# Token and channel mixing of the first two batches by halves, with the weight conversions spread further and the channel units set denser

## The chip, the cores and the metric

One core of a Trainium2 chip runs the whole program. The metric is device microseconds (us) of one execution.

## What is computed

Three layers follow one another on 4 batches of 448 tokens and 768 features (12 heads of 64). The reference, cut to its core:

```
attn = softmax(scale * q @ k^T, causal); x = attn @ v                # (4, 448, 768)
h  = relu(x^T @ w_tok1) @ w_tok2                                     # 448 -> 256 -> 448, over tokens
u  = x + h^T
x2 = u + relu(u @ w_ch1) @ w_ch2                                     # 768 -> 1536 -> 768, over channels
theta = x2 @ w_theta;  zr, zi = x2 * cos(theta), x2 * sin(theta)
y  = w_tok_r @ zr + w_tok_i @ zi
u2 = x2 + y
out = u2 + relu(u2 @ w_ch)
```

The weights arrive as 64-bit floats.

## The kernel before, in words

**Attention** runs in 168 steps: 4 batches, 6 pairs of heads, 7 score tiles each (`steps`). A step is a score matmul (L349, with L351 from the ninth pair on), a masked reduction on VectorE (L356), an exponential on ScalarE (L358), and later (LAG = 4 steps) the product with v (`pv`, L393 or L403). For pairs 0 to 11 the weights are transposed on TensorE (L365); from pair 12 (step 84) on they are split into two f16 parts (L378) and transposed by a DMA (L381, `pt<-ph`). After two pairs `tokmix` adds the token mixing and leaves two accumulator tiles `acc`; after six pairs a batch has its six.

**Channel units.** The layer `x2` is 96 units: for each batch and each half `fh` of the 1536 middle channels six units `ch1_unit` and six `ch2_unit`, in the order of the list `units`. A unit is 18 matmuls of 128x448 in f16 (L230 to L232, three products of a high and a low part), and needs one weight tile `ws` of 384 KB, loaded on SP's queue (L225, `stream_tile`) at most three units ahead. Units of a batch need its `ut` tiles: `split_ready` takes a power of two from the sum of squares of the six `acc` tiles (`power`: matmuls L136 and L138, two small VectorE operations, small GpSimd products L130 that give `p_u` and `s_u`), and then splits each `acc` (ScalarE L160 and VectorE L196). `UNIT_STEPS` says at which attention step each unit is written into the program; 69 units lie among the steps, the rest after them.

**Conversions.** 24 tiles of w_ch1 and w_ch2 are read as 64 bits (768 KB, tile `raw`, L173), rounded to f32 on VectorE (L183, L184, L185) after a ScalarE pass (L176, then squares L124), split in two f16 parts on GpSimd (L163) and VectorE (L196 `ws<-wf`) and stored for the units to load (`w_c<-ws`, L553). `ROUNDINGS` says at which step each begins; load, rounding, split and store come at fixed distances around that step. Six tiles of w_ch are converted late (`convert_late`). Conversions and units take their `ws` tiles from one ring of buffers.

The layer after it (`thetas`, `mix`, `out_unit`) follows the attention, mixed with the last units.

**Order.** Each engine executes its instructions in order; a scheduler sorts them by priority (`high_priority` moves an instruction forward) and by what they need, so that scores stand well ahead of the units that were written at the same step. SP's queue is one list as well: loads, stores and transposes start in its order.

Of the kernel before, what the change touches and what calls it, by code (L numbers as in the profile page):

```python
# [8 lines left out]
F32 = mybir.dt.float32  # L9
# [9 lines left out]
P = 128  # L19
B, H, S, D = 4, 12, 448, 64  # L20
E = H * D
NPR = H // 2
DT = E // P
# [2 lines left out]
FH = 6  # L26
NEG = -1.0e30
PSC = 32768.0
BUFS = dict(ut=12, h2=8, acc=12, ws=8, wf=3, raw=3, sb=3, ph=3, pt=5, t=3, junk=1)
NATIVE = {0, 1, 2, 3, 4, 5, 6, 7}  # L30
NATPV = {0, 1, 2, 3, 4, 5, 6, 7, 8, 9, 10, 11}
AHEAD, LAG, LOOK = 500, 4, 2
KEEP, UBACK = 6, 16
ROUND_BITS, ROUND_FETCH, ROUND_SPLIT, ROUND_STORE = 1, 2, 3, 5
LATE_CONVERT = 16
FIRST_UNIT, DENSE, RATE = 50, 88, (42, 29)
UNIT_STEPS = [FIRST_UNIT + n * (DENSE - FIRST_UNIT) // 14 if n < 14 else
              DENSE + -(-(n - 14) * RATE[0] // RATE[1]) for n in range(72)]
ROUNDINGS = [(at_step, n - 4) for n, at_step in enumerate((3, 4, 8, 9))] + [(14 + n * 78 // 23, n) for n in range(24)]
ENGINES = {  # L40
    0: dict(qhi="A", qlo="D", khi="A", klo="D", v="D", phi="A", xhi="A", xlo="D", uhi="A", ulo="D"),
}
# [12 lines left out]
def fused(ctx, tc, q, k, v, w_tok1, w_tok2, w_ch1, w_ch2, w_theta, w_tok, w_ch, out):  # L55
# [19 lines left out]
    main = ctx.enter_context(tc.tile_pool(name="main", bufs=2))  # L75
# [39 lines left out]
    p_w1, p_w2, p_wc = [table(f"p_w1{z}", 6) for z in range(2)], table("p_w2", 12), table("p_wc", 6)  # L115
# [13 lines left out]
    def product(dst, a, b, c):  # L129
        nc.gpsimd.tensor_scalar(out=dst, in0=a, scalar1=b, scalar2=c, op0=ALU.mult, op1=ALU.mult)  # L130

    def power(p, s, sq, unit=None):

        ps = mm_bank()
        n = sq.shape[-1]
        nc.tensor.matmul(ps[:, 0:1], lhsT=ones, rhs=tiny, start=True, stop=False)  # L136
        for j in range(n):
            nc.tensor.matmul(ps[:, 0:1], lhsT=ones, rhs=sq[:, j:j + 1], start=False, stop=j == n - 1)  # L138
        g = main.tile([P, 2], F32, tag="g", name="g", bufs=4)
        nc.vector.tensor_scalar(out=g[:, 0:1].bitcast(U32), in0=ps[:, 0:1].bitcast(U32), scalar1=1, scalar2=EXPONENT,  # L140
                                op0=ALU.logical_shift_right, op1=ALU.bitwise_and)
        two_over(g[:, 1:2], g[:, 0:1])
        product(s, g[:, 1:2], 2.0 ** -51, 1.0)
        if p is not None:
            product(p, g[:, 0:1], 2.0 ** 64, 1.0)
        if unit is not None:
            product(unit, g[:, 1:2], 2.0 ** -51, PSC)
# [304 lines left out]
    h2 = {}  # L452
# [2 lines left out]
    unit_end = [None]  # L455

    ready = set()

    def domain(b, fh):

# [22 lines left out]

    def ch2_unit(b, uT, acc, fh, d, w):
        ps = mm_bank()
        f = main.tile([P, 1], F32, tag="f", name="f", bufs=4)
        product(f, p_w2[:, fh * 6 + d:fh * 6 + d + 1], h_scale[0], 1.0)
        for ft in range(FH):
            unit_end[0] = mm3(ps[:, 0:S], w, h2[b, fh, ft], lambda a: a[:, ft * P:(ft + 1) * P], lambda a: a, ft == 0, ft == FH - 1)
        nc.vector.scalar_tensor_tensor(out=acc[d], in0=ps[:, 0:S], scalar=f, in1=acc[d], op0=ALU.mult, op1=ALU.add)  # L490
        if fh == 1:
            squares(sq_x[b][:, d:d + 1], acc[d])
            last_store[0] = nc.sync.dma_start(out=x2d[b][d], in_=acc[d])

    uTs = [[None] * DT for _ in range(B)]
    accs = [[None] * DT for _ in range(B)]
    units = [(b, fh, c, t) for b in range(B) for fh in range(2) for c in (1, 2) for t in range(6)]
    loaded = {}

    jobs = [((w_ch1, w_ch2)[c - 1][fh * 6 + t], wd[f"c{c}", fh, t],  # L500
             p_w1[fh][:, t:t + 1] if c == 1 else p_w2[:, fh * 6 + t:fh * 6 + t + 1]) for _, fh, c, t in units[:24]]
    late = [(w_ch[e], wd["c3", 0, e], p_wc[:, e:e + 1]) for e in range(DT)]

    def load_unit(n):
        if n < len(units) and n not in loaded and (n >= 24 or n in stored):
            b, fh, c, t = units[n]
            loaded[n] = stream_tile(wd[f"c{c}", fh, t])

    fetched, rounding, stored = {}, {}, set()
    at, halves = [0], [0]  # L510

    def split_ready():

        b = halves[0]
        if b < B and None not in accs[b]:
            s = s_u[:, b:b + 1]
            power(p_u[:, b:b + 1], s, sq_u[b])
            for d in range(DT):
                uTs[b][d] = hl_tile("ut")
                split_to(pick("uhi"), uTs[b][d], accs[b][d], s)  # L520
            halves[0] += 1
# [42 lines left out]
    def x_scale(b):  # L564
        power(p_x[:, b:b + 1], s_x[:, b:b + 1], sq_x[b])

    def run_units(n):
        for _ in range(n):
            u = at[0]
            load_unit(u)  # L570
            b, fh, c, t = units[u]
            if c == 1 and t == 0:
                h_scale[0] = domain(b, fh)
            if c == 1:
                ch1_unit(b, uTs[b], fh, t, loaded[u])
            else:
                ch2_unit(b, uTs[b], accs[b], fh, t, loaded[u])
            loaded[u] = None
            at[0] += 1
            for ahead in range(LOOK + (u >= 24)):  # L580
                load_unit(at[0] + ahead)
            if at[0] % 24 == 2 and 1 <= at[0] // 24 <= 3:
                x_scale(at[0] // 24 - 1)


    eng, turn = dict(ENGINES[0]), {}
# [392 lines left out]
```

## Time and profile before

| | |
|---|---|
| median of 3 runs | 893.53 us (893.36 to 894.15) |
| profiled execution | 893.95 us, of which 892.2 us is the span from the first to the last instruction |
| TensorE (PE) busy | 856.9 us, 96% |
| VectorE (DVE) busy | 631.9 us, 71% |
| ScalarE (ACT) busy | 543.7 us, 61% |
| granted TensorE clock, mean | 0.983 of full speed |

Matmuls are pipelined, so a matmul's own duration overlaps with the next one's, and a busy PE is not a PE at its peak. How fast PE works is read from the distance between the starts of consecutive matmuls.

### The profile page before, as it was taken

To read this page: it belongs to the slowest core of one execution; us is meant where nothing else is said; L and a number is where in the kernel's file an instruction comes from. 1 tells how busy PE (TensorE), PEld (TensorE's weight loads), DVE (VectorE), ACT (ScalarE), POOL (GpSimd) and SP (SyncE) were. 2 spreads that over 40 slices of the span, in tenths; PEclk is the share of its full clock that TensorE was granted. 3 is DMA by queue.
4 is the path that set the end of the run, shared out by engine and by line. 5 is a ranking of instruction groups with operands and counts; after the bars stand their busy time and mean duration, and the time that the engine had idled before them with its cause. 6 is when DMAs were issued, how large, how long until landed. Compare 5 with 4: busy or idle time off the path is not lost.

```text
span 892.2 us, 16092 instructions
## 1 busy us (share of the span) xinstructions
PE 856.9 (96%) x5619; PEld 551.0 (62%) x5619; DVE 631.9 (71%) x1511; ACT 543.7 (61%) x1271; POOL 180.9 (20%) x349
## 2 busy tenths in 40 slices
PE   7999789999979999999999989999999999999998
PEld 6888658786736656665656565555555555555554
DVE  6899957979998665767886358758856458566442
ACT  6798757767776663657664248447746447556441
POOL 2142322224142121211321111152111001101000
PEclk9999979999789999999999999999999999999999
DMA  7857846657699995767565679720621132231011
GB/s 225 250 181 236 289 168 215 238 198 220 150 337 300 289 213 145 187 165 179 150 194 146 188 248 303 241 72 20 193 89 56 60 115 62 72 116 57 18 50 73
DMA packets 105793, 149.63 MB, mean 168 GB/s; under 512 B 61104, under 2 KB 72304, under 8 KB 105712
## 3 DMA queue, kind: packets, MB, share of 16 engines
q1 hardware_dynamic: 105168, 147.59, 54.9%
q0 software_dynamic: 384, 0.79, 0.4%
q8 instruction: 44, 0.72, 0.3%
q10 hardware_dynamic: 160, 0.23, 0.1%
q14 instruction: 37, 0.30, 0.1%
HBM read 112.39 MB, written 22.81 MB: 152 GB/s over the span
## 4 chain that ended last, share of the span: by engine, by line
PE 71%; DVE 13%; DMA 8%; ACT 4%; issue 3%; POOL 2%; SPq 0%; DVEq 0%; ACTq 0%; POOLq 0%
PE ps_mm L230 16%; PE ps_mm L231 16%; PE ps_mm L232 16%; PE ps_pv L393 3%; PE ps_sc L349 3%; DMA ws<-w_c 3%; PE ps_sc L231 2%; PE ps_sc L230 2%; PE ps_sc L232 2%; DMA pt<-ph 2%; PE ps_mm L365 2%; DVE wf L184 1%; DVE sb L356 1%; PE ps_pv L403 1%; DVE ut L196 1%
## 5 line engine op out<-in xcount | busy, mean ns | idle before, releaser
L232 PE MATMUL ps_mm<-h,ws 128*128 128x448 f16 x432 | 152.1, 353 | 0.0
L231 PE MATMUL ps_mm<-h,ws 128*128 128x448 f16 x432 | 152.1, 353 | 0.0
L230 PE MATMUL ps_mm<-h,ws 128*128 128x448 f16 x432 | 151.6, 353 | 0.0
L230 PE MATMUL ps_mm<-ut,ws 128*128 128x448 f16 x288 | 104.5, 363 | 11.4 <-ACT ut L160 6.9
L230 PEld LDWEIGHTS <-ws 128*128 128x128 f16 x720 | 70.9, 98 | 69.3 <-DMA ws<-w_c 4.8
L232 PEld LDWEIGHTS <-ws 128*128 128x128 f16 x720 | 70.9, 99 | 65.4 <-issue 6.2
L358 ACT ACTIVATE sb<-sb,mx 128x192 f32<-128x192 f32 (+3 forms) x168 | 89.3, 533 | 35.5 <-DVE mx L356 31.5
L231 PEld LDWEIGHTS <-ws 128*128 128x128 f16 x720 | 70.8, 98 | 61.3 <-issue 4.3
L231 PE MATMUL ps_mm<-ut,ws 128*128 128x448 f16 x288 | 104.3, 362 | 1.2 <-DVE ut L196 1.2
L232 PE MATMUL ps_mm<-ut,ws 128*128 128x448 f16 x288 | 104.0, 361 | 0.0
L356 DVE CUSTOM_DVE_ANT_0 sb<-ps_sc,mask 128x192 f32<-128x192 f32 (+3 forms) x168 | 74.1, 454 | 13.5 <-PE ps_mm L365 10.1
L124 ACT ACTIVATE junk<-acc 128x448 bf16<-128x448 f32 x72 | 41.2, 572 | 63.8 <-DVE acc L871 40.8
L393 PE MATMUL ps_pv<-v_raw,ptf 128*128 128x128 f32 (+1 forms) x456 | 63.6, 277 | 1.0 <-DVE x L415 0.7
L160 ACT ACTIVATE ph<-sb 128x192 f16<-128x192 f32 (+3 forms) x84 | 36.2, 440 | 45.1 <-DMA pt<-ph 44.9
L378 DVE SCALAR_TENSOR_TENSOR ph<-sb,ph 128x64 f16<-128x64 f32 (+3 forms) x156 | 45.5, 335 | 25.6 <-ACT ph L160 25.2
L393 PEld LDWEIGHTS ps_pv<-v_raw,ptf 128*128 128x128 f32 x456 | 59.1, 193 | 6.0 <-PE ps_mm L138 1.5
L163 POOL TENSOR_SCALAR h<-t 128x448 f16<-128x448 f32 x48 | 33.0, 691 | 112.5 <-ACT t L476 107.0
L478 DVE TENSOR_TENSOR h<-t,h 128x448 f16<-128x448 f32 x48 | 32.0, 669 | 24.5 <-POOL h L163 24.5
L349 PE MATMUL ps_sc<-kh,qs 128*128 128x256 f32 (+2 forms) x112 | 45.7, 413 | 3.3 <-DVE mx L356 3.1
L130 POOL TENSOR_SCALAR f<-p_w,c_h 128x1 f32<-128x1 f32 x48 | 21.5, 450 | 126.7 <-DVE acc L490 91.6
L476 ACT ACTIVATE t<-ps_mm,c_scale 128x448 f32<-128x448 f32 x48 | 29.7, 621 | 28.3 <-PE ps_mm L232 25.2
L230 PE MATMUL ps_sc<-th,ut 128*128 128x384 f16 x144 | 47.0, 326 | 0.0
(215 smaller groups left out, 2096.1 us busy)
## 6 DMA issues: line engine op xcount, KB each, us to landing
ws<-w_c SPq DMA_DIRECT2D x120, 384.0 KB, 4.5
raw<-in_w_ch_dram SPq DMA_DIRECT2D x30, 768.0 KB, 5.0
w_c<-ws SPq DMA_DIRECT2D x30, 384.0 KB, 3.6
q_raw<-in_q_dram SPq DMA_DIRECT2D x16, 448.0 KB, 4.0
k_raw<-in_k_dram SPq DMA_DIRECT2D x16, 448.0 KB, 5.3
v_raw<-in_v_dram SPq DMA_DIRECT2D x24, 288.0 KB, 3.3
x2d<-acc SPq DMA_DIRECT2D x24, 224.0 KB, 3.1
acc<-x2d SPq DMA_DIRECT2D x24, 224.0 KB, 3.1
```

Source lines behind the costliest of these rows:

```text
L124: nc.scalar.activation(j[:, 0:src.shape[-1]], src, AF.Square, accum_out=dst)
L160: nc.scalar.activation(dst, src, AF.Copy, scale=scale)
L163: e.tensor_scalar(out=dst, in0=src, scalar1=scale, scalar2=0.0, op0=ALU.mult, op1=ALU.add)
L230: nc.tensor.matmul(ps, lhsT=ka(a[:, 0]), rhs=kb(b[:, 0]), start=first, stop=False)
L231: nc.tensor.matmul(ps, lhsT=ka(a[:, 0]), rhs=kb(b[:, 1]), start=False, stop=False)
L232: return nc.tensor.matmul(ps, lhsT=ka(a[:, 1]), rhs=kb(b[:, 0]), start=False, stop=last)
L349: nc.tensor.matmul(ps[:, 0:n], lhsT=lhs, rhs=cut(pp.kh), start=True, stop=pp.kl is None)
L356: pp.first = nc.vector.tensor_tensor_reduce(out=dst, in0=src, in1=msk, op0=ALU.add, op1=ALU.min, scale=-0.125, scalar=3.0e38, accum_out=pp ...
L358: pp.last = nc.scalar.activation(sb[:, 0:kk], sb[:, 0:kk], AF.Exp, bias=pp.mx[:, j:j + 1], scale=-1.0, accum_out=pp.sm[:, j:j + 1])
L378: nc.vector.scalar_tensor_tensor(out=dst, in0=sb[:, c0:c1], scalar=PSC, in1=hi[:, c0:c1], op0=ALU.mult, op1=ALU.subtract)
L393: pp.pv = nc.tensor.matmul(pp.ps[:, reg:reg + n], lhsT=pt[:, u], rhs=pp.v[0][:, vt * D:vt * D + n], start=(u == 0), stop=(u == len(blks) - 1))
L478: gates[0] = nc.vector.tensor_tensor(out=t[:, 1], in0=f, in1=t[:, 0], op=ALU.subtract)
```

## The change

- The units of batches 0 and 1 run by halves: batch 0 first half, batch 1 first half, batch 0 second half, batch 1 second half (`HALVES`). Batches 2 and 3 stay as they were. The second half's weights are therefore needed 12 units later.
- The 24 conversions begin at steps 14 to 111 (`CONVERTED`) where they began at steps 14 to 92.
- 12 units stand at steps 53 to 89, 36 at steps 93 to 131, 21 at steps 135 to 165. Before, 14 stood at steps 50 to 87 and one every 1.45 steps from step 88 on.
- 16 buffers for `acc` where there were 12; 7 for `ws` where there were 8; 2 for `raw` where there were 3.
- `split_ready`'s `power` gets high priority, and from batch 1 on the six scales `f` of a half are one GpSimd product.

```diff
-BUFS = dict(ut=12, h2=8, acc=12, ws=8, wf=3, raw=3, sb=3, ph=3, pt=5, t=3, junk=1)
+BUFS = dict(ut=12, h2=8, acc=16, ws=7, wf=3, raw=2, sb=3, ph=3, pt=5, t=3, junk=1)
...
-ROUNDINGS = [(at_step, n - 4) for n, at_step in enumerate((3, 4, 8, 9))] + [(14 + n * 78 // 23, n) for n in range(24)]
+FIRST_UNIT = 53
+UNIT_STEPS = [FIRST_UNIT + n * 10 // 3 for n in range(12)] + [93 + n * 11 // 10 for n in range(36)] + [135 + n * 3 // 2 for n in range(21)]
+CONVERTED = [14 + 6 * n for n in range(6)] + [49 + 5 * n for n in range(6)] + [78 + n * 19 // 5 for n in range(6)] + [99 + n * 5 // 2 for n in range(6)]
...
+HALVES = ((0, 0), (1, 0), (0, 1), (1, 1), (2, 0), (2, 1), (3, 0), (3, 1))
...
-        f = main.tile([P, 1], F32, tag="f", name="f", bufs=4)
-        product(f, p_w2[:, fh * 6 + d:fh * 6 + d + 1], h_scale[0], 1.0)
+        if b == 0:
+            f = main.tile([P, 1], F32, tag="f", name="f", bufs=4)
+            product(f, p_w2[:, fh * 6 + d:fh * 6 + d + 1], h_scale[0], 1.0)
+        else:
+            if d == 0:
+                f_six[0] = main.tile([P, DT], F32, tag="f6", name="f6", bufs=2)
+                product(f_six[0], p_w2[:, fh * 6:fh * 6 + 6], h_scale[0], 1.0)
+            f = f_six[0][:, d:d + 1]
...
-    units = [(b, fh, c, t) for b in range(B) for fh in range(2) for c in (1, 2) for t in range(6)]
+    units = [(b, fh, c, t) for b, fh in HALVES for c in (1, 2) for t in range(6)]
...
-            power(p_u[:, b:b + 1], s, sq_u[b])
+            with tc.high_priority(AHEAD):
+                power(p_u[:, b:b + 1], s, sq_u[b])
...
-            if at[0] % 24 == 2 and 1 <= at[0] // 24 <= 3:
-                x_scale(at[0] // 24 - 1)
+            if u >= 2 and units[u - 2][1:] == (1, 2, 5):
+                x_scale(units[u - 2][0])
```

`load_unit` and `jobs` follow the new order: a unit's weights are loaded once the conversion of that tile is stored.

Three places show the order that results. The first is VectorE's list just ahead of the first unit, around the first splits into `ut` (the `ws<-wf` rows are the ends of conversions, `wf` alone is rounding). Before:

```order
L196 SCALAR_TENSOR_TENSOR ws_1368<-wf_1224,s_1369,ws_1368 128x768
L183 TENSOR_SCALAR wf_1524<-wf_1524 128x768
L410 TENSOR_TENSOR x0_188<-ps_pv_1282,sm_1174 128x384
L415 TENSOR_SCALAR x0_188<-ps_pv_1282,sm_1174 64x64 x2
L184 SCALAR_TENSOR_TENSOR wf_1524<-raw_1210,wf_1524 128x768
L140 TENSOR_SCALAR g_1407<-ps_mm_1399 128x1
L185 SCALAR_TENSOR_TENSOR wf_1524<-raw_1210,wf_1524 128x768
L127 TENSOR_SCALAR g_1407<-g_1407 128x1
...
L196 SCALAR_TENSOR_TENSOR ws_1471<-wf_1364,s_1472,ws_1471 128x768
L196 SCALAR_TENSOR_TENSOR ut_1412<-acc_579,s_u_149,ut_1412 128x448
```

and now:

```order
L411 TENSOR_TENSOR x0_188<-ps_pv_1188,sm_1101 128x384
L141 TENSOR_SCALAR g_1301<-ps_mm_1293 128x1
L416 TENSOR_SCALAR x0_188<-ps_pv_1188,sm_1101 64x64 x2
L168 TENSOR_TENSOR qs_1523<-q_raw_1517,qs_1523 64x896
L197 SCALAR_TENSOR_TENSOR ws_1268<-wf_1143,s_1269,ws_1268 128x768
L128 TENSOR_SCALAR g_1301<-g_1301 128x1
...
L168 TENSOR_TENSOR xg1_1405<-x0_188,xg0_1404 128x4x128
L197 SCALAR_TENSOR_TENSOR ut_1306<-acc_569,s_u_149,ut_1306 128x448
```

The whole rounding of a tile (`wf_1524`) and the end of one more conversion have left this place; in the list up to the first `ut` split 11 conversions were complete and now 6 are.

The second is GpSimd's list at the same place, where `s_u` is the scale that the splits wait for. Before:

```order
L130 TENSOR_SCALAR p_u_148<-g_1407 128x1
L130 TENSOR_SCALAR c_h_1487<-p_fh_147,p_u_148 128x1
L130 TENSOR_SCALAR f_2083<-p_w2_143,c_h_1487 128x1
L130 TENSOR_SCALAR f_2169<-p_w2_143,c_h_1487 128x1
L130 TENSOR_SCALAR f_2249<-p_w2_143,c_h_1487 128x1
L130 TENSOR_SCALAR f_2408<-p_w2_143,c_h_1487 128x1
L130 TENSOR_SCALAR s_u_149<-g_1407 128x1
```

and now:

```order
L131 TENSOR_SCALAR c1_scale0_145<-p_w10_141,two_fh0_1437 128x6
L131 TENSOR_SCALAR p_u_148<-g_1301 128x1
L131 TENSOR_SCALAR c_h_1441<-p_fh_147,p_u_148 128x1
L131 TENSOR_SCALAR s_u_149<-g_1301 128x1
L131 TENSOR_SCALAR p_w2_143<-g_1418 128x1
```

Four products `f` no longer stand ahead of `s_u`.

The third is SP's queue where the last of the 24 conversions (`w_c2_1_5`) is stored and loaded again by a unit. Before:

```order
L553 DMA w_c2_1_5_116<-ws_3322 128x1536
L493 DMA x2d0_0_69<-acc_579 128x448
L381 DMA_TRANSPOSE pt_3709<-ph_3705 128x7x128
L381 DMA_TRANSPOSE pt_3755<-ph_3751 128x7x128
L493 DMA x2d0_1_70<-acc_596 128x448
L225 DMA ws_3498<-w_c2_1_5_116 128x1536
```

and now:

```order
L226 DMA ws_4075<-w_c2_1_3_114 128x1536
L565 DMA w_c2_1_4_115<-ws_4038 128x1536
L501 DMA x2d0_0_69<-acc_569 128x448
L382 DMA_TRANSPOSE pt_4659<-ph_4655 128x5x128
L174 DMA raw_6093<-in_w_ch_dram 128x1536
L501 DMA x2d0_1_70<-acc_586 128x448
L226 DMA ws_4213<-w_c2_1_4_115 128x1536
L565 DMA w_c2_1_5_116<-ws_4147 128x1536
L226 DMA ws_4333<-w_c2_1_5_116 128x1536
```

The load that served the 24th unit now serves the 36th, and it stands directly behind the store it reads.

## Rows read from the trace of the kernel before

**Rows 1.** The page's head: span, then busy time of two engines.

```profile
span 892.2 us, 16092 instructions
PE 856.9 (96%) x5619; PEld 551.0 (62%) x5619; DVE 631.9 (71%) x1511; ACT 543.7 (61%) x1271; POOL 180.9 (20%) x349
```

**Rows 2.** PE's timeline: start, length, line, tiles, idle before and its releaser.

```profile
112.80 0.53 PE L230 MATMUL ps_mm<-ut,ws 128*128 128x448 f16 x1 [4.67 <-ACT ut L160]
...
115.97 0.53 PE L231 MATMUL ps_mm<-ut,ws 128*128 128x448 f16 x1 [1.20 <-DVE ut L196]
...
116.67 0.58 PE L230 MATMUL ps_mm<-ut,ws 128*128 128x448 f16 x1
117.04 0.58 PE L231 MATMUL ps_mm<-ut,ws 128*128 128x448 f16 x1
...
123.55 0.35 PE L232 MATMUL ps_mm<-ut,ws 128*128 128x448 f16 x1
123.74 0.35 PE L230 MATMUL ps_mm<-ut,ws 128*128 128x448 f16 x1
...
354.96 0.35 PE L230 MATMUL ps_mm<-h,ws 128*128 128x448 f16 x1
```

**Rows 3.** Busy time by stretch, with granted clock, DMA share and rate.

```profile
core 0: us, PE busy (x) PEld busy (x) DVE busy (x) ACT busy (x) POOL busy (x), PEclk, DMA share, GB/s
0.00:20.00 20.00, 15.19 (x86) 12.54 (x87) 12.94 (x49) 12.94 (x37) 5.33 (x17) 1.00 0.79 235
20.00:100.00 80.00, 76.93 (x551) 67.06 (x550) 74.59 (x191) 65.18 (x178) 24.39 (x38) 1.00 0.70 230
100.00:120.00 20.00, 13.40 (x74) 8.77 (x73) 17.02 (x39) 16.58 (x38) 7.75 (x13) 0.78 0.83 291
120.00:220.00 100.00, 100.00 (x692) 77.07 (x691) 77.70 (x192) 67.16 (x168) 30.41 (x46) 0.99 0.60 201
220.00:260.00 40.00, 30.28 (x216) 21.01 (x214) 38.00 (x98) 32.08 (x78) 12.31 (x18) 0.81 0.82 219
260.00:340.00 80.00, 78.51 (x596) 50.24 (x595) 60.45 (x172) 45.40 (x118) 15.35 (x31) 0.99 1.02 273
540.00:892.20 352.20, 347.65 (x1987) 192.08 (x1985) 219.04 (x427) 192.29 (x382) 47.90 (x103) 1.00 0.30 97
```

**Rows 4.** The same view, from the start to one point each.

```profile
0.00:112.80 112.80, 99.52 (x689) 85.46 (x690) 98.44 (x266) 89.11 (x241) 36.10 (x67) 0.99 0.74 237
0.00:340.00 340.00, 314.31 (x2207) 236.69 (x2208) 280.71 (x737) 239.33 (x614) 95.53 (x162) 0.96 0.77 234
```

**Rows 5.** Groups by line and shape: what one conversion costs; busy, mean ns, idle before.

```profile
L196 DVE SCALAR_TENSOR_TENSOR ws<-wf,s,ws 128x768 f16<-128x768 f32 x30 | 30.7, 1023 | 8.9 <-POOL ws L163 6.9 <-ACT ws L160 1.8
L184 DVE SCALAR_TENSOR_TENSOR wf<-raw,wf 128x768 uint32<-128x768 uint32 x30 | 30.2, 1006 | 0.3
L185 DVE SCALAR_TENSOR_TENSOR wf<-raw,wf 128x768 uint32<-128x768 uint32 x30 | 29.1, 971 | 0.2
L183 DVE TENSOR_SCALAR wf<-wf 128x768 uint32<-128x768 uint32 x30 | 20.4, 680 | 1.4 <-ACT wf L176 1.2
L176 ACT ACTIVATE wf<-raw 128x768 f32<-128x768 f32 x30 | 27.3, 910 | 3.6 <-DVE ws L196 3.5
L124 ACT ACTIVATE junk<-wf 128x768 bf16<-128x768 f32 x30 | 25.2, 838 | 3.4 <-DVE wf L185 2.8 <-DVE g L127 0.4
```

**Rows 6.** GpSimd's timeline at the first unit.

```profile
110.43 1.47 POOL L130 TENSOR_SCALAR f<-p_w,c_h 128x1 f32<-128x1 f32 x4
111.86 0.19 POOL L130 TENSOR_SCALAR s_u<-g 128x1 f32<-128x1 f32 x1
```

**Rows 7.** The chain that ended last, around unit 16.

```profile
246.34 10.03 DMA ws<-w_c
```

**Rows 8.** DMA issues: count, KB each, median us from issue to landing.

```profile
ws<-w_c SPq DMA_DIRECT2D x120, 384.0 KB, 4.5
w_c<-ws SPq DMA_DIRECT2D x30, 384.0 KB, 3.6
```

More of the change, by code (lines that the diff above doesn't have):

```diff
@@ L35 @@
 LATE_CONVERT = 16
-FIRST_UNIT, DENSE, RATE = 50, 88, (42, 29)
-UNIT_STEPS = [FIRST_UNIT + n * (DENSE - FIRST_UNIT) // 14 if n < 14 else
-              DENSE + -(-(n - 14) * RATE[0] // RATE[1]) for n in range(72)]
-ROUNDINGS = [(at_step, n - 4) for n, at_step in enumerate((3, 4, 8, 9))] + [(14 + n * 78 // 23, n) for n in range(24)]
+FIRST_UNIT = 53
+UNIT_STEPS = [FIRST_UNIT + n * 10 // 3 for n in range(12)] + [93 + n * 11 // 10 for n in range(36)] + [135 + n * 3 // 2 for n in range(21)]
+CONVERTED = [14 + 6 * n for n in range(6)] + [49 + 5 * n for n in range(6)] + [78 + n * 19 // 5 for n in range(6)] + [99 + n * 5 // 2 for n in range(6)]
+ROUNDINGS = [(at_step, n - 4) for n, at_step in enumerate((3, 4, 8, 9))] + [(at_step, n) for n, at_step in enumerate(CONVERTED)]
+HALVES = ((0, 0), (1, 0), (0, 1), (1, 1), (2, 0), (2, 1), (3, 0), (3, 1))
 ENGINES = {
@@ L457, in fused @@
     ready = set()
+    f_six = [None]
     def domain(b, fh):
@@ L496, in fused @@
     accs = [[None] * DT for _ in range(B)]
-    units = [(b, fh, c, t) for b in range(B) for fh in range(2) for c in (1, 2) for t in range(6)]
+    units = [(b, fh, c, t) for b, fh in HALVES for c in (1, 2) for t in range(6)]
     loaded = {}
     jobs = [((w_ch1, w_ch2)[c - 1][fh * 6 + t], wd[f"c{c}", fh, t],
-             p_w1[fh][:, t:t + 1] if c == 1 else p_w2[:, fh * 6 + t:fh * 6 + t + 1]) for _, fh, c, t in units[:24]]
+             p_w1[fh][:, t:t + 1] if c == 1 else p_w2[:, fh * 6 + t:fh * 6 + t + 1])
+            for fh in range(2) for c in (1, 2) for t in range(6)]
     late = [(w_ch[e], wd["c3", 0, e], p_wc[:, e:e + 1]) for e in range(DT)]
     def load_unit(n):
-        if n < len(units) and n not in loaded and (n >= 24 or n in stored):
-            b, fh, c, t = units[n]
+        if n >= len(units) or n in loaded:
+            return
+        b, fh, c, t = units[n]
+        if fh * 12 + c * 6 - 6 + t in stored:
             loaded[n] = stream_tile(wd[f"c{c}", fh, t])
```

## The prediction

> **What bounds the kernel now.** The page's head comes first: PE is busy 96% of the span [rows 1], which seems to leave nothing to win. [...] I counted every matmul at its spacing at full clock: 2664 of this kind at 0.189 us make 503.5, 504 of 384 columns at 0.162 make 81.6, 816 f32 ones of 128 columns at about 0.11 make 89, and the remaining 1635 small ones make 109 us. PE's work is therefore 783.7 us, and 108.5 us of the span are lost: PE stood, was fed thinly, or ran at half clock. I call this "lost time", and follow it by the start of each unit (18 matmuls, 3.4 us).
>
> When unit 0 starts, at 112.8, PE has done 61.9 us of work, so 50.9 are lost. When unit 35 starts, at 354.96 [rows 2], it has done 262.6, so 92.3 are lost. By unit 75 it is 103.0, and only 5.4 come after. From 540 on VectorE (DVE) has 219 us of work in 352 and PE loses almost nothing [rows 3]. So the tail cannot be improved, and everything is decided in the first 355 us.
>
> The table of stretches says what holds PE up there [rows 3]. From 20 to 100 DVE is busy 74.6 of 80 us: it is the bound, with ACT at 65.2. At 100 to 120 DVE is busy 17.0 of 20; PE waits 4.67 and 1.20 us for the `ut` splits [rows 2] and runs at half clock behind that (0.78 in the row). From 120 to 220 DVE has slack, 77.7 of 100, and PE is the bound. From 220 to 260 DVE is the bound again, 38.0 of 40, and PE gets too little; a wait of 10.03 us for a weight load ends this stretch [rows 7]. So the load alternates: DVE is full while PE starves, and then the reverse.
>
> **The change, part by part.** *Conversions.* One costs DVE 0.68 + 1.01 + 0.97 + 1.02 = 3.68 us and ACT 0.91 + 0.84 = 1.75 us, small operations aside [rows 5]. Five fewer of them are complete ahead of unit 0: DVE is relieved of 18.4 us there, ACT of 8.7. DVE had 98.4 us of work by 112.8, ACT 89.1 [rows 4]. As DVE was the bound, up to 18 us of time could go; as ACT takes part in the same steps and then becomes the busier of the two, it may be only 9. I take 13.
>
> *The scale `s_u`.* Four products of 1.47 us together leave the place ahead of it [rows 6], and its matmuls rank higher. That is 1.5 us of the wait, and up to 5 us more if PE's standing becomes too short to lose the clock. I take 3 in all.
>
> *`acc`, `f` in one product, `HALVES`.* 16 buffers hold two batches and two thirds of a third; GpSimd, which has the fewer and larger products, is busy 181 us of 892 [rows 1]. Both cost nothing. The cover of the buffers is that batch 0 is finished (unit 35) before the third mixing of batch 2 needs its tiles; if not, `tokmix` waits one unit, 3.4 us.
>
> *From unit 2 on.* I sum DVE's work in its new order, each instruction at its mean duration. (Done for the kernel before, this count gives the measured 98.4 at unit 0.) Batch 1's splits, which unit 12 needs, end at 193 us of DVE work; the last of the 24 conversions ends at 281. In the kernel before they ended at 223 and at 236. To get the time, DVE's idle time is added. Up to unit 12 I expect 7.1 idle in the first 20 us, as now [rows 3]; 10 up to unit 0, against 5.4 now, as ACT shares the bound (bounds 5 and 16); 3 around unit 0, as in 100 to 120; 8 in the 92 us of work up to unit 12, where DVE has more to do than PE (92 against 81): between the 5% idle of 220 to 260 [rows 3] and the 17% of the first 340 us [rows 4]. That is 28, so unit 12 starts at about 193 + 28 = 221 us. PE has then done 156.6, so 64 are lost; the kernel before had lost about 75 at that much work.
>
> *From unit 12 to unit 35.* PE has 105 us of work here, DVE 88. At the end unit 35 waits for the last conversion: a store of 3.6 and a load of 4.5 us [rows 8] behind DVE's 281, so 97 in all. PE's 105 is the larger, and the usual small gaps add 4: 109 is one end. The other end is the DMA. SP's queue holds, between the loads of units 12 and 35, 23 unit loads, 11 stores, 11 `raw` loads, 15 loads of q, k and v, 2 stores of x2 and 36 transposes: 33.9 MB, where it held 31.5. The row that comes nearest to a full DMA moved 273 GB/s at a share of 1.02 [rows 3]; at that rate 33.9 MB take 124 us. [...] The row is one of mixed transposes, as this stretch is, but the trace does not show that it could not have gone faster, so I take 114, one third of the way: unit 35 starts at about 335, with 73 us lost against 92.3 now.
>
> *After unit 35.* PE has 522 us of work left, and I leave the losses as they are: 10.7 up to unit 75 and 5.4 behind. That is 335 + 522 + 16 = 873 us of span. The profiled execution took 893.95, 1.75 more than its span, and the median of the runs is 0.42 below that one; so the forecast is **874.5 us**, 19 us (2.1%) less. Of these, 16 come ahead of unit 2 (13 + 3), 5 are given back up to unit 12, where DVE is the bound, and 8 to 9 are won from there to unit 35, where PE now lost 14 or more, the long wait for weights among them.
>
> **The rivals.** *The DMA fills (slower than forecast, still faster than before).* From unit 12 to 35 the stretch takes 124 to 130 us. For it: the share of 1.02, and the 10.03 us landing behind three `raw` loads [rows 7]. Against it: two `raw` buffers let fewer loads pile up. Time: 884 to 891.
>
> *ACT holds the first stretch.* Only 5 of the 16 us ahead of unit 2 come: 885. Against it: ACT was at 65 of 80 with the conversions still in it [rows 3].
>
> *Better.* DVE idles 20 up to unit 12 and the second stretch takes its 109: 861.
>
> *Slower than before: the ring of `ws`.* It has 7 buffers, and unit loads now come three ahead in a dense row of 36 units, between which 11 conversions want a buffer each for their split. A conversion that finds none holds GpSimd (L163) and then DVE (L196), with the masked reductions of the scores queued behind it on DVE, so that PE loses its scores too. With 8 buffers the splits of 30 conversions waited 8.9 us on DVE in all [rows 5], which speaks against it. If each of the 11 waits for one unit, 3.4 us, that is 37 us: 912. It decides from six such waits on (20 us).
>
> *Slower by the clock.* PE gets only 50 us of work in some 80 us before unit 12 is dense. [...] If the clock were low throughout, these 50 us would take 100: 895. [...]
>
> **How the numbers follow.** Forecast case (866 to 883): 0.50. DMA or ACT (883 to 892): 0.21. Better (below 866): 0.12. No measurable change: 0.04. Slower: 0.13, of which the ring 0.09 and the clock 0.04. A measurement of this kernel tells 0.2% (1.8 us) from no change. Faster is 0.50 + 0.21 + 0.12 = 0.83. The best bounds (unit 12 at 212, 109 behind it, the rest as now) give 861, the worst that still win 892. The range 859 to 892 leaves some 0.05 below and 0.15 to 0.17 above.
>
> **What the profile would show.** Right: unit 0 starts near 98 to 102 with ACT above 85% ahead of it; no wait of 4 us for `ut`; unit 12 near 221; unit 35 near 335; no loss in the tail. DMA: waits of PE for `ws<-w_c` of several us between 220 and 340 at a share near 1. Ring: idle time of L163 and L196 on `ws` of 20 us or more. Clock: a row of 0.5 to 0.8 between 170 and 250. The prediction is wrong above all if the losses after unit 35 do not stay at 16: PE then runs some 20 us ahead, and DVE, which must finish batch 2's splits before unit 48, has that much less time.

## The result, and the profile after

The changed kernel takes 900.84 us (median of 5 runs, 898.67 to 903.62); the kernel before took 893.72 beside it. The ratio is 1.0084 (95%: 1.0064 to 1.0104): slower by 0.8%, where 874.5 us and faster were forecast. The profiled execution took 900.77 us. Medians here and below are of all executions, while the ratios leave out one slow execution each of `e1_conv_old` (991.82 us; the other five have a median of 905.59) and of `p3_before_natpv14` (3141.0 us). The head of the profiled execution's page has, as before [rows 1], one span and the busy times:

```profile
span 898.9 us, 16042 instructions
PE 856.7 (95%) x5619; PEld 550.2 (61%) x5619; DVE 633.0 (70%) x1511; ACT 544.2 (61%) x1271; POOL 168.6 (19%) x319
```

The work is the same; the span is 6.7 us longer, and PE stands for it. The table of stretches shows where (columns as in [rows 3] and [rows 4]):

```profile
0.00:20.00 20.00, 14.60 (x83) 12.10 (x84) 12.72 (x48) 13.32 (x37) 5.35 (x17) 1.00 0.66 197
20.00:100.00 80.00, 76.16 (x555) 67.79 (x553) 57.98 (x167) 60.61 (x169) 15.99 (x25) 1.00 0.53 167
100.00:120.00 20.00, 19.75 (x132) 14.62 (x133) 19.92 (x51) 18.05 (x47) 8.45 (x12) 1.00 0.79 265
120.00:220.00 100.00, 95.86 (x696) 75.83 (x695) 82.94 (x209) 73.06 (x183) 21.08 (x38) 0.98 0.67 211
220.00:260.00 40.00, 31.33 (x239) 19.33 (x237) 37.79 (x103) 28.25 (x72) 12.43 (x20) 0.83 0.85 223
260.00:340.00 80.00, 74.56 (x490) 44.34 (x491) 65.83 (x154) 41.64 (x95) 23.98 (x39) 0.94 0.90 259
540.00:898.90 358.90, 352.06 (x2013) 194.36 (x2012) 224.84 (x437) 197.98 (x394) 46.78 (x96) 1.00 0.31 101
0.00:109.47 109.47, 100.06 (x707) 87.84 (x708) 80.09 (x243) 82.79 (x229) 26.22 (x51) 1.00 0.59 182
0.00:231.97 231.97, 211.44 (x1511) 174.17 (x1511) 185.44 (x506) 173.74 (x455) 55.83 (x101) 0.97 0.63 198
```

From 20 to 100 DVE has 16.6 us less to do than before, and PE gains nothing there. From 100 to 120 the gain is real: PE busy 19.75 for 13.40, the clock at 1.00 for 0.78. From 120 on it is given back: 4 us of standing by 220, and a clock of 0.83 until 260, 0.81 before; from 260 to 340 0.94 for 0.99.

PE's timeline after, to set against [rows 2]: the first line is unit 0, the last two are units 12 and 35.

```profile
109.47 0.36 PE L231 MATMUL ps_mm<-ut,ws 128*128 128x448 f16 x1
...
205.11 0.20 PE L404 MATMUL ps_pv<-v_hi,pt 128*128 128x64 f16 x1 [2.25 <-DMA pt<-ph]
...
225.04 0.21 PE L404 MATMUL ps_pv<-v_raw,pt 128*128 128x64 f16 x1 [2.87 <-DVE v_raw L318]
...
230.86 0.24 PE L404 MATMUL ps_pv<-v_hi,pt 128*128 128x64 f16 x1 [3.06 <-DMA pt<-ph]
...
231.97 0.97 PE L231 MATMUL ps_mm<-ut,ws 128*128 128x448 f16 x2
...
355.64 0.35 PE L231 MATMUL ps_mm<-h,ws 128*128 128x448 f16 x1
```

Unit 0 starts without the wait of 4.67 us. Unit 10 starts at 197.10, unit 11 at 217.15 and unit 12, batch 1's first, only at 231.97: PE has little but attention steps in this time, and they wait, longest for their transposes. I call this the hole. PE's waits from 190 to 262, with their sum, number and longest:

```profile
PE ps_pv L404 <- DMA pt<-ph: 6.6, 5, 3.1
PE ps_pv L404 <- DVE v_raw L318: 2.9, 1, 2.9
PE ps_sc L350 <- DVE mx L357: 2.0, 4, 0.9
PE ps_pv L404 <- DVE x L416: 0.9, 1, 0.9
```

These waits make 12.4 us. The half clock seen in this time (from 235.2 to 236.7 the granted clock was 0.50 and f16 matmuls of 128x448 started 0.37 us apart, from 237.4 to 239 1.00 and 0.19; a mean of 0.87 from 190 to 262, row below) costs up to 0.13 x 72 = 9 us more, an estimate, and less where PE waits anyway.

**Lost time, counted again.** I redid the prediction's count with a spacing for every kind of matmul: the lower quartile of the distances between starts in the kernel before. PE's work is 823.5 us in both kernels, not 783.7, so before lost 69 us in all and not 108.5. Time lost at the same amount of PE work:

```
PE work done     100   170   220   302 (unit 35)   end
before          27.1  28.6  48.2  53.0             68.7
after           17.0  19.7  45.5  54.7             75.4
```

The change wins 10.1 us by 100 us of work, gives 7.4 back by 220, 4.4 more by unit 35 and 5.1 behind it: together the 6.7 of the spans. The mark at 220 lies on a jump of the changed kernel, and finer marks show where the time is given back. The hole costs 18.7 us up to unit 13 (180 to 200 us of work), as much as the kernel before loses at its units 13 to 17 (18.8, from 185 to 215): at 215 the change is still some 9 us ahead. It then loses 7.3 us at 258 to 268, around unit 17, and 4.3 at 301 to 306, where unit 24 waits 1.8 for its weights; the granted clock falls to half at both (0.50 from 262.7 to 267.5 and from 302 to 304.5). The row of the first, and PE's longest wait in it:

```profile
256.00:270.00 14.00, 10.15 (x57) 5.20 (x56) 11.44 (x32) 9.23 (x21) 2.04 (x4) 0.76 0.90 231
...
PE ps_mm L231 <- ACT qs L161: 2.1, 1, 2.1
```

### The profile page after: what moved, and what is told of

It reads as the page before. It is cut to its first block, busy times and chain, and to the rows that moved or that the text cites. A ratio compares the mean times of both kernels' runs of the same rounds, so it can differ in the third digit from the quotient of the medians.

```text
span 898.9 us, 16042 instructions
## 1 busy us (share of the span) xinstructions
PE 856.7 (95%) x5619; PEld 550.2 (61%) x5619; DVE 633.0 (70%) x1511; ACT 544.2 (61%) x1271; POOL 168.6 (19%) x319
## 4 chain that ended last, share of the span: by engine, by line
PE 70%; DMA 13%; DVE 7%; ACT 5%; issue 2%; SPq 1%; POOL 1%; ACTq 0%; DVEq 0%; POOLq 0%
PE ps_mm L231 16%; PE ps_mm L233 16%; PE ps_mm L232 15%; DMA pt<-ph 7%; PE ps_pv L394 3%; PE ps_sc L350 3%; PE ps_sc L231 3%; PE ps_sc L232 3%; PE ps_sc L233 3%; DMA ws<-w_c 2%; PE ps_mm L366 2%; DVE sb L357 1%; PE ps_sc L352 1%; PE ps_pv L404 1%; DVE ph L379 1%
## 5 line engine op out<-in xcount | busy, mean ns | idle before, releaser
L359 ACT ACTIVATE sb<-sb,mx 128x320 f32<-128x320 f32 (+3 forms) x168 | 89.2, 532 | 17.8 <-DVE mx L357 15.6
L357 DVE CUSTOM_DVE_ANT_0 sb<-ps_sc,mask 128x320 f32<-128x320 f32 (+3 forms) x168 | 74.5, 455 | 9.2 <-PE ps_mm L366 5.2
L164 POOL TENSOR_SCALAR h<-t 128x448 f16<-128x448 f32 x48 | 34.8, 728 | 149.1 <-ACT t L478 148.9
L498 DVE SCALAR_TENSOR_TENSOR acc<-ps_mm,f,acc 128x448 f32<-128x448 f32 x48 | 32.5, 678 | 21.6 <-PE ps_mm L233 21.4
L883 DVE SCALAR_TENSOR_TENSOR acc<-ps_mm,mix_scale,acc 128x448 f32<-128x448 f32 x24 | 16.4, 683 | 44.2 <-PE ps_mm L233 44.0
L231 PE MATMUL ps_sc<-th,ut 128*128 128x384 f16 x144 | 46.9, 326 | 0.0
L233 PE MATMUL ps_sc<-th,ut 128*128 128x384 f16 x144 | 46.8, 326 | 0.0
```

Of the source, the lines that this page charges most:

```text
L164: e.tensor_scalar(out=dst, in0=src, scalar1=scale, scalar2=0.0, op0=ALU.mult, op1=ALU.add)
L231: nc.tensor.matmul(ps, lhsT=ka(a[:, 0]), rhs=kb(b[:, 0]), start=first, stop=False)
L233: return nc.tensor.matmul(ps, lhsT=ka(a[:, 1]), rhs=kb(b[:, 0]), start=False, stop=last)
L357: pp.first = nc.vector.tensor_tensor_reduce(out=dst, in0=src, in1=msk, op0=ALU.add, op1=ALU.min, scale=-0.125, scalar=3.0e38, accum_out=pp ...
L359: pp.last = nc.scalar.activation(sb[:, 0:kk], sb[:, 0:kk], AF.Exp, bias=pp.mx[:, j:j + 1], scale=-1.0, accum_out=pp.sm[:, j:j + 1])
```

## The experiments

Ratios are to the kernel before on the same chip, with 95% intervals. "Lost" is the time lost when PE has done that much work, counted as above in the profiled execution, and "then" what is lost from 220 to 820. Runs with `NATPV` raised do 9.4 (two pairs) or 14.1 us (three pairs) more PE work. The profiled execution can lie several us from the median (n2's is 5.7 above, p1's 4.3 above), and what it lost carries that.

```
                     median  ratio [95%]             lost: 100   170   220  then
before               893.72  1                            27.1  28.6  48.2  16.1
after                900.84  1.0084 [1.0064, 1.0104]      17.0  19.7  45.5  25.4
e1_conv_old          908.25  1.0144 [1.0095, 1.0192]      29.0  34.1  53.0  20.7
e2_units_old         917.90  1.0241 [1.0204, 1.0277]      22.9  25.3  65.2  25.5
e3_ws8               903.30  1.0086 [1.0057, 1.0114]      18.9  21.6  47.7  29.9
e4_small             896.90  1.0019 [1.0001, 1.0037]      25.2  26.7  45.7  19.9
f1_no_halves         904.06  1.0092 [1.0067, 1.0117]      29.6  35.1  49.1  26.2
a1_spread            906.74  1.0118 [1.0089, 1.0147]      16.0  20.4  46.3  31.2
g1_thin              898.63  1.0029 [1.0011, 1.0047]      20.5  23.6  46.8  23.1
n1_before_noround    886.73  0.9909 [0.9882, 0.9936]      20.5  22.1  35.3  21.6
n2_after_noround     896.17  1.0017 [0.9993, 1.0042]      16.5  19.3  39.3  32.9
p1_natpv15           897.14  1.0018 [0.9992, 1.0045]      19.8  22.2  25.6  31.4
p2_lag6              915.94  1.0236 [1.0208, 1.0264]      28.5  30.9  49.6  39.5
q1_after_poolq       911.44  1.0178 [1.0158, 1.0197]      23.9  26.3  49.1  32.0
q2_before_poolq      897.26  1.0012 [0.9988, 1.0036]      22.1  23.7  42.9  27.0
p3_before_natpv15    894.68  0.9993 [0.9979, 1.0006]      26.9  28.4  30.4  18.2
t3_p3_places         895.51  1.0009 [0.9994, 1.0024]      25.9  29.3  31.2  20.0
t1_f1_natpv15        900.02  1.0037 [1.0004, 1.0070]      30.2  35.4  37.3  20.1
t2_e1_natpv15        899.72  1.0058 [1.0038, 1.0079]      29.3  34.2  39.2  16.4
p3_before_natpv14    891.49  0.9954 [0.9940, 0.9969]      26.8  28.3  30.3  22.2
```

### One part undone

e1_conv_old is the changed kernel with the conversions at the steps of before:

```diff
-... + [(at_step, n) for n, at_step in enumerate(CONVERTED)]
+... + [(14 + n * 78 // 23, n) for n in range(24)]
```

> The changed kernel with the 24 conversions begun at steps 14 to 92 again; the rest of the change stays. Theory M (the work was moved to the wrong place): up to about 190 us PE has little idle time to give, since its f32 matmuls of the first 12 pairs fill it, so relieving VectorE there wins 9 us at most, while from 190 to 262 us VectorE is the bound and each conversion moved there costs time. Then this kernel loses 4 to 6 us ahead of unit 9 and wins 8 to 12 between units 9 and 36: 895 us or less. Theory U (the units): batch 0's second half no longer fills PE from step 84 to 100, because batch 1's first half must wait for its splits; then the conversions matter little and this kernel takes 899 to 904. Theory R (the smaller rings of weight and raw tiles): 899 to 903.

Unit 0 starts at 118.57 and the kernel is slower still, by 0.6%, just more than the two intervals allow for chance. Theory M, which had 895 or less, is refuted: spreading the conversions helps.

e2_units_old has units at the density of before (where 14 stood at steps 50 to 85), 12 and then 57:

```diff
+UNIT_STEPS = [50 + n * 38 // 14 for n in range(12)] + [91 + n * 42 // 31 for n in range(57)]
```

> The changed kernel with the units at about the steps of before: 12 from step 50 to 79, then 57 at 1.35 steps from step 91, in the new order by halves. Theory M: the sparse stretch between unit 9 and unit 12 stays bound by VectorE, so 898 to 903. Theory U: the places of the units are what starves PE; but as the order by halves stays, the gap before step 91 grows by three units, so if the density from step 93 on was the harm it falls to 895 or less, and if the gap was, it rises to 905 or more. Theory R: 899 to 903.

Unit 12 comes at 250.85, 40 us behind unit 11, which itself has waited 10.5 us for its weights. The denser places are needed once the units run by halves.

e3_ws8 gives `ws` its eighth buffer back (`acc=14, ws=8`):

> The changed kernel with 8 buffers for the weight tiles as before, and 14 for acc in exchange for the room. Theory R: the waits for weight buffers and the waits of the transposes queued behind them on SP shrink, 894 to 896. Theories M and U: 899 to 902.

Nothing changes. As `acc` is smaller here too, the changed kernel's own row says it more directly: the 30 splits of conversions on DVE waited 8.3 us in all, 8.9 before [rows 5], for GpSimd and ACT, and the 24 on GpSimd 2.1.

```profile
L164 POOL TENSOR_SCALAR ws<-wf,s 128x768 f16<-128x768 f32 x24 | 28.8, 1199 | 2.1
...
L197 DVE SCALAR_TENSOR_TENSOR ws<-wf,s,ws 128x768 f16<-128x768 f32 x30 | 30.8, 1026 | 8.3 <-POOL ws L164 5.5 <-ACT ws L161 2.6
```

The ring of `ws` is not the cause.

e4_small is the kernel before with the high priority of `power` and the one product for six scales:

> The kernel before with the two small parts alone: the high priority of the power in split_ready, and the six scales f in one product from batch 1 on. By the prediction the scale comes 1.5 us earlier and the clock may stay up, so 889 to 892. By theory M these parts are worth what PE stood at unit 0: its waits of 4.67 and 1.20 us there shrink, and 3 to 6 us less remain at unit 2, of which part is given back later: 889 to 893. If the splits come no earlier: 893 to 894.

0.2% slower, at most 0.4%, where a gain was expected: 1.9 us are won by 100 us of work, of the 3 that the prediction gave these parts, and 3.8 are lost after 220.

f1_no_halves is e1_conv_old with the order of units of before:

```diff
-    units = [(b, fh, c, t) for b, fh in HALVES for c in (1, 2) for t in range(6)]
+    units = [(b, fh, c, t) for b in range(B) for fh in range(2) for c in (1, 2) for t in range(6)]
```

> The kernel of the previous run with conversions begun at 14 to 92, with the order of the units of before as well (batch 0 whole, then batch 1): places of the units and rings are those of the change, the order by halves is not. Theory H (the order by halves is the harm: PE has no unit to run between the last unit of batch 0's first half and the splits of batch 1): the loss between 170 and 200 us of PE work falls from 18 us to 10 or less, and the run takes 890 to 897 against 908 for its counterpart. Rival P (the places are the harm: 12 units up to step 89, none from 90 to 92): the loss stays at 15 or more, and 903 to 908. Rival B (the smaller rings make PE lose more between 250 and 400 us of work): that loss stays at 13 to 18 where it was 9 before, whatever happens ahead of it.

The gap ahead of unit 12 closes (234.58, 5.1 us behind unit 11), and the loss between 170 and 200 falls as theory H says, but not the time: some 7 us are lost anew between units 13 and 15, so that 49.1 are lost at 220, where e1 has 53.0. The order decides where the gap lies more than how large it is.

a1_spread spreads the first 12 units to step 97, over the hole; g1_thin is e4_small with six conversions thinned out ahead of unit 0:

```diff
+UNIT_STEPS = [FIRST_UNIT + n * 4 for n in range(12)] + [98 + n * 12 // 13 for n in range(36)] + ...   # a1
+ROUNDINGS = ... + [(14 + 6 * n if n < 6 else 50 + (n - 6) * 42 // 17, n) for n in range(24)]           # g1
```

> The changed kernel with its first 12 units spread over steps 53 to 97 instead of 53 to 89 and the next 36 over steps 98 to 130. Theory H: two or three units now fill PE where it starved; as VectorE has slack from 120 to 190, little is lost there, and the loss between 170 and 200 us of PE work falls from 19 to 12 or 14: 894 to 898. If instead VectorE and the transposes set the pace of the attention steps there and the units only wait their turn: 900 to 904.

> The kernel before with its order, places and rings, with the two small parts, and with the conversions thinned as in the change up to step 44 (6 of them) and the other 18 at 2.47 steps each from step 50 to 92. Theory H: thinning alone is what was good in the change. The standing at unit 0 falls (loss at 100 us of PE work from 27 to 17 or 20), VectorE has room for the moved ones from 120 to 220, and the rest stays as before: 884 to 889. If the moved conversions push VectorE's full stretch earlier instead, all of it is given back by unit 15: 892 to 896.

Neither gains; both end at or just beyond the slower of their two forecasts. Of these kernels, whatever had been won by 100, all but e2 and e1 stand at 45 to 50 us lost by 220.

### VectorE's rounding left out

In n1_before_noround and n2_after_noround the 24 conversions skip the rounding, 64 us of DVE:

```diff
-        round64(f, fetched.pop(j)[1])
+        raw = fetched.pop(j)[1]
+        if n < 0:
+            round64(f, raw)
```

> The kernel before, with the 24 conversions not rounded: the three VectorE products of L183 to L185 (0.68 + 1.01 + 0.97 = 2.66 us) are left out for them, 64 us of VectorE in all, so the output differs. It asks how much time ahead of unit 0 VectorE's load can give back at all. By the prediction's count (50.9 us lost at unit 0, VectorE the bound) the 11 conversions ahead of unit 0 free 29 us and unit 0 comes at 84 to 95. By the corrected count (PE lost 22 us there, some 7 of them in the start) no relief of VectorE can bring it much: unit 0 at 98 to 104, and the whole run gains 5 to 20 us.

> The changed kernel with the same rounding left out for the 24 conversions, 64 us of VectorE, so the output differs. Theory D: the loss at 190 to 262 (45 us in all at 220 us of PE work) is VectorE's volume of conversions in front of batch 1's splits; without rounding unit 12 comes 15 us or more earlier (below 217), the loss at 220 us of PE work is 25 to 32, the span 875 to 885. Theory T: it is the chain of the attention steps (exponential, split, DMA transpose, product with v) with no units to fill it; unit 12 comes less than 8 us earlier, the loss at 220 stays above 38, the span is 888 or more.

The stretches of n1 from 20 to 100 and up to unit 0, and unit 0 on PE:

```profile
20.00:100.00 80.00, 78.70 (x573) 69.47 (x572) 50.12 (x167) 66.50 (x185) 21.51 (x38) 1.00 0.82 250
...
0.00:108.87 108.87, 99.53 (x690) 85.81 (x691) 68.18 (x228) 86.75 (x238) 30.91 (x68) 1.00 0.78 234
...
108.87 0.35 PE L230 MATMUL ps_mm<-ut,ws 128*128 128x448 f16 x1 [1.75 <-ACT ut L160]
```

DVE is relieved of 30.3 us ahead of unit 0 (68.18 against 98.44 in [rows 4]), and unit 0 comes 3.9 us earlier. That refutes the prediction's reading of this stretch, and is even less than the second count allowed (98 to 104). By 100 us of work 6.6 us are won, and the whole run, with 64 us less for DVE, is 0.9% faster (8 us). n2 up to unit 12, and unit 12 on PE:

```profile
0.00:229.13 229.13, 209.86 (x1501) 173.99 (x1502) 146.24 (x452) 170.91 (x452) 49.97 (x101) 0.98 0.66 200
...
229.13 0.53 PE L231 MATMUL ps_mm<-ut,ws 128*128 128x448 f16 x1 [2.36 <-DMA w_c<-ws]
```

DVE has 39 us less to do ahead of unit 12 (146.24 against 185.44), and unit 12 comes 2.8 us earlier, or 5.2 without its wait for a conversion's store: less than 8 either way. The loss at 220 is 39.3, above theory T's 38. So the volume of DVE (theory D) does not open the gap; the chain of the steps (theory T) is what is left, and the next runs test it. By the ratios n2 is some 6 us faster than the changed kernel.

### Transposes on PE

p1_natpv15 has three more pairs transposed on PE, p2_lag6 two more steps between score and product:

```diff
-NATPV = {0, 1, 2, 3, 4, 5, 6, 7, 8, 9, 10, 11}
+NATPV = set(range(15))             # p1
-AHEAD, LAG, LOOK = 500, 4, 2
+AHEAD, LAG, LOOK = 500, 6, 2       # p2, with ph=4, pt=6, ws=6
```

> The changed kernel with the weights of pairs 12, 13 and 14 (steps 84 to 104) transposed on PE as those of pairs 0 to 11, not split and sent through a DMA transpose: 21 DMA transposes, 21 splits on ScalarE and VectorE fewer; PE does some 10 us more work. Theory T: these steps' waits for the transposes open the gap; unit 12 comes 8 us or more earlier (below 224), the wait of the product with v for the transposes falls from 7.6 us to below 4, and the time is 890 to 898. Theory D: VectorE's volume decides; it is relieved by some 15 us of splits, unit 12 comes earlier by 3 to 8 us, the waits go to the scores, and the time is 897 to 905.

> The changed kernel with the product with v six steps behind its score in place of four (four ph and six pt buffers, and six ws buffers to make room, which cost nothing at seven against eight). Theory T: the transposes have two more steps to land; the waits of the product with v for them fall from 7.6 us to below 3, and the time falls by 3 to 6 us, to 895 to 898. Theory D: the waits go to the scores and to the splits, as VectorE's order is as full as before; the loss at 220 us of PE work stays at 43 to 48, the time at 899 to 905.

The stretch from 190 to 262 in five kernels. Changed kernel, then p1:

```profile
190.00:262.00 72.00, 58.20 (x437) 39.25 (x435) 68.17 (x189) 52.05 (x132) 19.43 (x33) 0.87 0.87 236
```
```profile
190.00:262.00 72.00, 70.61 (x476) 51.19 (x475) 59.09 (x135) 49.33 (x117) 17.91 (x31) 1.00 0.68 238
```

n2 (no rounding), then the kernel before, then p3_before_natpv14 (below):

```profile
190.00:262.00 72.00, 60.27 (x458) 41.02 (x457) 56.72 (x166) 54.41 (x137) 15.27 (x32) 0.91 0.97 252
```
```profile
190.00:262.00 72.00, 62.28 (x426) 43.48 (x425) 65.58 (x166) 53.92 (x133) 24.03 (x37) 0.88 0.75 216
```
```profile
190.00:262.00 72.00, 71.38 (x490) 52.59 (x489) 59.33 (x139) 51.35 (x124) 22.59 (x38) 1.00 0.58 202
```

With the three pairs on PE the gap is gone: PE 70.61 of 72, clock 1.00, unit 12 at 223.43, 3.4 us lost between 170 and 220 of work where the changed kernel loses 25.8. Of the 22.4 us that are no longer lost, 14.1 pay for the added work, and unit 12 comes 8.5 us earlier. With n2's DVE as lightly loaded as p1's (56.72 and 59.09), PE still stands, so it is not the relief of DVE that fills the gap, but the way through the DMA that these steps no longer take (21 splits on ACT go with it, and were not taken away by themselves). p2 is 2.4% slower, beyond both forecasts, and still waits 7.7 us for the transposes from 190 to 262. It decides nothing: it has lost 11.5 us more than the changed kernel by 100 us of work, ahead of the first DMA transpose, and has a `ws` buffer less. Why was not followed up.

### Conversions off SP's queue

q1 and q2 issue the 24 stores (L565, L553) and all 64-bit loads (L174, L173; 60, those of the other weights too) from GpSimd, in the changed kernel and in the one before. The stores' edit in q1 (the loads' is alike):

```diff
-            nc.sync.dma_start(out=jobs[n][1], in_=rounding.pop(j))
+            nc.gpsimd.dma_start(out=jobs[n][1], in_=rounding.pop(j))
```

> The changed kernel with the conversions' 64-bit loads and their stores issued by GpSimd in place of SP's queue. Theory S (SP's queue is held by conversions that wait for VectorE, 17.5 us at the stores and 9.7 us at the loads between 262 and 420, and the transposes behind them come late): the loss after 220 us of PE work falls from 25 to 15 to 19 us, the waits of the scores from 8.0 to below 5, and the time to 891 to 896. Theory T2 (the step's chain is slow by itself, or SP's waits are idle time that nothing needs): the loss after 220 stays at 22 to 30, the time at 897 to 905.

> The kernel before with the same loads and stores on GpSimd's queue. Theory S: its conversions end by 300 us and SP is held by them for some 10 us at 190 to 262; it gains less than the changed kernel, 0 to 4 us, 890 to 894. Theory T2: no change, 892 to 897.

q1 is 1.8% slower, q2 the same. The waits of the scores from 262 to 420 are 4.6 us, against 3.2 in the changed kernel (not 8.0, as expected of it), so theory S finds no support. But now GpSimd's list is held: from 190 to 262 it waits 13.9 us at the loads and 9.3 at the stores, and q1 has lost 6.9 us more by 100 us of work. So the runs show that this move does not pay, not that SP's waits are free.

### Who owns the later loss

p3 is the kernel before with `NATPV` up to pair 14. t3 adds the new places, t1 also the buffers, the high priority and the one product, t2 also the order by halves; p1 adds the new steps of the conversions and is the whole change.

> The kernel before with the weights of pairs 12 to 14 transposed on PE, 14 us more PE work as in the changed kernel. There it took 22 us of loss out of 170 to 220 us of PE work and the time fell by some 5 us. In the kernel before the loss there is 19.4, of which up to 15 could go. If the gap is worth as much here: 889 to 895. If the kernel before does not need it, because its gap is shorter and half of it is the end of the conversions: 896 to 905, the 14 us of work in part on top.

> The kernel before with pairs 12 to 14 transposed on PE (p3, which lost 18 us after 220 us of PE work and took 894.7) and the changed kernel's UNIT_STEPS alone. If the denser places (36 units in 38 steps, then 21 in 32) own the later loss, it rises to 26 to 32 and the time to 901 to 908; if not, it stays at 16 to 21 and the time at 892 to 898.

> As the one before, and with the changed kernel's buffers (acc 16, ws 7, raw 2), the high priority of power and the scales in one product; order of units and conversions are those of before. If the buffers, raw above all, own the later loss: 26 to 32 us after 220 us of PE work. If not: the same as with the places alone, to 3 us.

> As the one before, with the order by halves. If the halves own the later loss: it rises by 6 us or more over the run without halves, to 26 to 32. If neither places, buffers nor halves do, the conversions at steps 14 to 111 are left: this run then loses under 22 there, against 31 with them.

After 220 of work p3 loses 18.2, t3 20.0, t1 20.1, t2 16.4 and p1 31.4. Only the last step, the conversions, raises the later loss, by 15 us; it also lowers the loss up to 220 by 13.6 (39.2 to 25.6). The 15 are an upper figure: p1's profiled execution took 901.4 us, 4.3 above its median, and t2's is its median. The stretch from 262 to 420 in t2, then p1:

```profile
262.00:420.00 158.00, 156.94 (x1121) 101.27 (x1119) 98.26 (x270) 86.94 (x224) 18.61 (x39) 1.00 0.68 183
```
```profile
262.00:420.00 158.00, 147.84 (x1053) 93.78 (x1052) 114.58 (x291) 88.18 (x221) 34.00 (x60) 0.99 0.81 223
```

The conversions that have moved there bring DVE 16 us, GpSimd 15 us and the DMA 40 GB/s more, and PE stands 9 us more. In time the step is still worth 0.4% (1.0058 to 1.0018); the other parts cost a little each: places 0.16%, buffers and high priority 0.28%, halves 0.21%, single differences that the intervals hardly separate. Taken together, the change costs 0.25% where pairs 12 to 14 are on PE (0.9993 to 1.0018) and 0.84% where their transposes are DMAs: most of the slowdown hangs on these transposes.

### A version that beats both

The kernel before, with two pairs (12 and 13) on PE and no part of the change:

> The kernel before with the weights of pairs 12 and 13 transposed on PE: 9.4 us more PE work, where three pairs took 14.1 and removed 17 us of loss between 170 and 220. If two pairs still close the gap, 888 to 893; if the gap moves to the next pair's transposes, 893 to 898.

891.49 us against 894.73, ratio 0.9954 (0.9940 to 0.9969). From 190 to 262 PE is busy 71.38 of 72 at full clock (its row is above), and one wait is left there:

```profile
PE ps_mm L429 <- DVE xg L167: 0.6, 1, 0.6
```

The loss between 170 and 220 falls from 19.6 to 2.0 us for 9.4 us of work; 6 us of the rest are lost later. In the kernel before PE itself waits only 1.4 us for transposes from 190 to 262, but 4.4 for a weight load, which SP issues at 246.34, after seven transposes that take up its queue from 230 to 243. Which of the two the change of two pairs cures was not separated.

## Why the prediction was wrong

**The step that failed is the count of PE's work**: "the remaining 1635 small ones make 109 us". They make 149. Among them are 752 f32 matmuls of 192 to 448 columns, hardly small, which at their own spacing take 122 us. Two of them on PE's timeline of the changed kernel, a score of the first pairs:

```profile
33.35 0.92 PE L350 MATMUL ps_sc<-k_pad,q_raw 128*128 128x448 f32 x2
34.10 0.27 PE L366 MATMUL ps_mm<-ident,sb 128*128 128x128 f32 x1
```

Two starts take 0.75 us, 0.375 each, where an f16 matmul of the same shape, the kind of the 2664 in the count, takes 0.19 (at 123.55 in [rows 2], where the granted clock was 1.00; at 116.67 it was 0.50 and the starts 0.37 apart). Of the 40 us, 29 lie ahead of unit 0: PE had done 90.7 us of work there, not 61.9, and lost 22.1, not 50.9; 14 of these in the first 94 us, half of them before 20. So "DVE is the bound" from 20 to 100 was wrong: PE itself was, with some 8 of the 80 us lost, and DVE at 74.6 of 80 was nearly full without holding it much. PE's busy share says little here (96%, with 69 us of 892 lost), and DVE's no more: 30 us of relief ahead of unit 0 brought it forward by 3.9 (n1).

**By stretches** (forecast, then measured): up to unit 0 100 and 109.5; to unit 12 121 and 122.5; to unit 35 114 and 123.7; to the end 538 and 543.3. These are 873 and 898.9. The changed kernel from unit 2 to unit 12:

```profile
124.13:231.97 107.84, 97.11 (x716) 76.54 (x715) 91.01 (x235) 77.75 (x196) 26.05 (x47) 0.94 0.66 207
```

- *Conversions, "I take 13", and `s_u`, 3.* DVE's relief was right to a fraction of a us (98.4 - 18.4 = 80.0, measured 80.09). But DVE then idled 29.4 us ahead of unit 0, not 17: there were only some 13 us to win after the start, of which 10 came (by 100 us of work). No wait for `ut` and no half clock at 110 (1.00 from 100 to 120): as forecast. The "up to 5 us more" for the clock was my estimate; in the changed kernel the clock was 0.50 behind waits of 2.13 us (at 262.75) and 1.82 (at 301.39) too. ACT was busy 76% of the time ahead of unit 0 (82.79 of 109.47), not above 85%.
- *Up to unit 12, "5 given back".* The time was nearly right by luck, for a wrong reason. From unit 2 to unit 12 DVE had the work that I counted (91.01 us, forecast 92), but PE had 90, not 81, and the stretch took 107.84 where I had 100 (the row above). DVE idled 46.5 us up to unit 12, not 28: the stretch was not DVE's, as n2 confirms, but that of steps whose products wait for transposes while few units stand between. I costed `HALVES` at nothing; f1 and t2 put the order by itself at no more than a few us, but it sets where this hole lies.
- *From unit 12 to 35, 114.* PE's 105 us of work were right (105.3); 18.4 were lost, not 4 to 9, and this is where the lead is given back. The time is near the forecast's DMA end of 124, but PE waits for `ws<-w_c` only 1.8 us in the whole run: the DMA rival has the time and hardly the mechanism. Behind unit 12 come two more half-clock stretches (the two at 0.50 named above; 0.94 from 260 to 340), waits of scores for DVE (3.2 us from 262 to 420) and single waits for splits. The 10.03 us that I took for a wait of the kernel before are the load's length on the chain; PE waited 4.4 for it.
- *After unit 35, "I leave the losses as they are".* By the second count they were 15.7 and became 20.8. The sign that I named for being wrong came true, but not by the path that I named: PE was not 20 us ahead (unit 35 at 355.64, before at 354.96).
- *Rivals.* The ring is refuted by e3 and the splits' row. The clock is a part, not the cause: 0.83 from 220 to 260 stands against 0.81 before. The ACT rival's 885 was still too low. Slower had a chance of 0.13, and neither of the two paths that I gave it is the one that came.

**What stays open:** which resource of the moved conversions makes the later loss. DVE's rounding (n2) and the `ws` buffers (e3) are each not it alone; q1 does not clear SP's queue, as GpSimd lost by it, and the transfers and GpSimd's work were not taken away by themselves.

## What to carry to other kernels

Before pricing relief for a busy engine, count what the engine that waits has lost in that stretch, with a measured spacing for every kind of instruction; the relief cannot win more than that. Work that leaves one stretch lands in another: price the stretch that takes it, too. A hole in the busiest engine that waits for a chain through three others was closed more cheaply here by doing that chain's step on the engine that waits (9.4 us of work for 17.6 us of loss) than by moving the order of everything around it.

## What the runs showed of the hardware that was not expected

- An f32 matmul of 128x448 on `k_pad` takes two records of 0.375 us, where `kl` (the round f32 type in the code, printed as f32 too) takes one of about 0.20 in the kernel before, and f16 0.19.
- The DMA transposes (`pt<-ph`) landed 4.0 us after their issue from 190 to 262 of the changed kernel (median of 25; 6.5 at most) and held SP's queue about 1.2 us each, so that one pair's seven take some 8 us of the queue (an estimate, 7 x 1.2). The view of tile `pt` in that stretch:

```profile
L382 SPq DMA_TRANSPOSE pt<-ph x25: 1169/1201/1938, 192.5 to 261.9; - x25
...
DMA to landing us min/median/max: 2.3/4.0/6.5
```
